# Moving the local exponentials and one chunk's transposes in a hand-planned attention kernel

## The chip, the cores and the metric

The kernel runs on one core of one Trainium2 chip. The time is device microseconds of one execution. Before the change three runs gave 905.56, 906.0 and 906.24 us, median 906.0. The profiled execution took 906.4 us, of which 904.6 us are the span from its first to its last instruction.

## The reference

Two attentions over the same x (2048 positions, width 448, 16 heads of 28) are mixed by a gate per position:

```
q, k, v = x @ A_wqkv                      # A: local and dilated
logits  = q[s] . k[s - 2*w], w = 0..7     # 8 keys per position, masked where s - 2*w < 0
a = (softmax(logits * scale) . v[s - 2*w]) @ A_wo
q, k, v = x @ B_wqkv                      # B: full attention
b = (softmax(q @ k.T * scale) @ v) @ B_wo
out = g * a + (1 - g) * b,   g = sigmoid(sum(x * gate_w))
```

## The kernel before

All is float32, with products split into high and low parts. First come the projections (to about 254 us). Then follow 256 **steps**. The full attention B is cut into 16 units (4 groups of 4 heads by 4 blocks of 512 queries), numbered u = 0 to 15, and each unit into 16 steps kt, one for each block of 128 keys; step st = 16u + kt. In every step TensorE makes the scores of four heads (line 1041), ScalarE turns them into exponentials in two instructions of 128x1024 (line 1044), and TensorE multiplies the exponentials of the step before with V into the bank `av` (line 995). Beside it TensorE makes, up to step 234, three tiles of scores for units to come (line 144), of which VectorE takes the maxima (lines 148 and 174); the maxima go through ScalarE (lines 179, 180), GpSimd (line 181), a VectorE transpose (line 186) and SyncE to DRAM, and serve as the offsets of the later exponentials. The first exponential of a step is taken here as the step's start: step 0 starts at 254.29 us, step 80 at 435.60, step 96 at 471.78.

A unit's output is finished in the steps behind it, at fixed places (`hooks`, filled by `at`): with f = 16(u+1), ScalarE copies `av` to `osb` ahead of the scores of step f+1 (position "pre", line 854), SyncE stores and reloads the row sums, VectorE takes the reciprocal at f+6 (line 867), GpSimd scales it (line 868), SyncE stores it and, at the end of step f+8, loads it back spread over the partitions as `rbc` (line 877); GpSimd multiplies `osb` by `rbc` at the end of step f+12 (`fin_on`, line 906), ScalarE rounds that at "pre" of step f+18 in most units (`fin_hi`, line 910), GpSimd takes the rest (`fin_lo`, line 914), and SyncE stores both at f+22. All DMAs of these steps are issued on SyncE's queue, in program order.

The local attention A runs in the same steps, mostly on GpSimd and VectorE, in 8 **chunks** c = 0 to 7 of two heads (the seventh chunk is c = 6). Its pieces are: loads of q, k and v on SyncE ("ld"); eight products of q with shifted k on GpSimd (`a_score`, item "s", c, w; line 616, for odd w with a folding addition, line 621), each summed by VectorE in 2 or 4 reduces (`a_reduce`, item "r", line 626); a softmax in nine items "m", c, 0 to 8 (`a_softmax`), of which number 4 is the exponential on ScalarE (line 642); eight products with v and seven additions on GpSimd (`a_av`, item "a", c, w, part; lines 665 and 670), of which ("a", c, 7, 1) is the last sum of the chunk; four VectorE transposes (`a_turn`, item "t", line 674); and four pairs of stores on SyncE (`a_store`, "st", line 680).

These pieces are placed by a planner that runs when the program is written out (`issue`). Each engine has a list sorted by a due place. In each step `issue` goes through an engine's list and takes the first item whose needs were issued at least `lag` steps earlier; for GpSimd and VectorE it adds the item's written cost to the engine's backlog `late` and stops when the backlog would pass a limit (4.2 us for GpSimd, 0.7 us for VectorE). At the end of a step the backlog falls by 2.25 us, and VectorE's rises by what the maxima cost. So a placed item changes the room for the items after it, and every later placement can move. Each engine then runs its instructions strictly in the order in which they were written out: in a step first SyncE's items, then GpSimd's, then the scores, VectorE's hooks and items, ScalarE's items, the product with V, and the hooks at "end".

When all items are placed, the output projection's weights are split and the last steps (from 235) take the output products of both attentions.

Of the kernel before, what the change touches and what calls it, by code (L numbers as in the profile page):

```python
# [17 lines left out]
W, DIL = 8, 2  # L18
# [7 lines left out]
def gated_mix_kernel(ctx: ExitStack, tc: tile.TileContext, xT, xn, gw, wA, wB, woAB, out):  # L26
# [179 lines left out]
    with tc.tile_pool(name="xp", bufs=1) as xp, tc.tile_pool(name="wp", bufs=2) as wp:  # L206
# [203 lines left out]
        r, t = xst[:, 0, 0:3, :], xst[:, 0, 3, :]  # L410
# [40 lines left out]
        for n, t in enumerate(tiles):  # L451
# [4 lines left out]
            for w in splits:  # L456
                i, k = (n - splits[w][0]) * splits[w][1], splits[w][1]
# [36 lines left out]
            if parts and parts[0][0] <= n:  # L494
                _, u, t = parts.pop(0)
# [23 lines left out]
    hooks = {}  # L519
# [4 lines left out]
    def run(pos, st):  # L524
        for f in hooks.pop((st, pos), ()):
            f()
# [69 lines left out]
    for nme in ("k", "v"):  # L596
        for i in range(2):
            t = a1.tile([128, HALO + NJ, 56], F32, name=f"{nme}t{i}")
# [3 lines left out]
    def a_load(c, nme):  # L602
        if nme == "q":
            qt[c] = a2.tile([128, NJ, 56], F32, name="qt")
            nc.sync.dma_start(qt[c], a_own[0][c])
        else:
            t = kvt[nme, c % 2]
            i = 1 if nme == "k" else 2
            nc.sync.dma_start(t[:, 0:HALO, :], a_prev[i][c, :, NJ - HALO:NJ, :])
            nc.sync.dma_start(t[:, HALO:, :], a_own[i][c])  # L610

    def a_score(c, w):
        if w == 0:
            Lt[c] = a2.tile([128, W, NJ, 2], F32, name="L", bufs=3)
        p = a3.tile([128, NJ, 56], F32, tag="prod", name="prod")
        nc.gpsimd.tensor_tensor(out=p, in0=qt[c], in1=kvt["k", c % 2][:, HALO - DIL * w:HALO - DIL * w + NJ, :],  # L616
                                op=ALU.mult)
        prods[c, w] = p.rearrange("p j (h d) -> p (j h) d", d=DH)
        if NR[c, w] == 2:
            lo, hi = prods[c, w][:, :, 0:DH // 2], prods[c, w][:, :, DH // 2:]  # L620
            nc.gpsimd.tensor_tensor(out=lo, in0=lo, in1=hi, op=ALU.add)  # L621
            prods[c, w] = lo

    def a_reduce(c, w, i, n):
        r = slice(2 * NJ // n * i, 2 * NJ // n * (i + 1))
        nc.vector.tensor_reduce(Lt[c][:, w].rearrange("p j h -> p (j h)")[:, r], prods[c, w][:, r], axis=X, op=ALU.add)
# [45 lines left out]
    def a_turn(c, i):  # L672
        r = slice(4 * i, 4 * i + 4)
        nc.vector.transpose(oatT[:, r].rearrange("p j h e -> p (j h e)"),
                            oats[c % 2][:, r].rearrange("p j h e -> p (j h e)"))

    def a_store(c, a):
        for h in range(2):
            f = 56 * c + DH * h
            nc.sync.dma_start(oa_scr[f:f + DH].rearrange("f (j p) -> f j p", j=NJ)[:, :, 32 * a:32 * a + 32],  # L680
                              oatT[32 * a:32 * a + DH, :, h, :])
# [6 lines left out]
    def item(eng, key, name, cost, needs, f):  # L688
        lists[eng].append((key, name, cost, needs, f))
# [6 lines left out]
    for c in range(8):  # L696
        c0 = CH * c
        for nme in "qkv":
            item("sp", c0 if nme != "v" else c0 + 18, ("ld", nme, c), 0,
                 [(("s", c - 2, 7), 3)] if nme != "v" else [(("a", c - 2, 7, 1), 3)],  # L700
                 lambda c=c, nme=nme: a_load(c, nme))
        for w, o in enumerate((0, 2, 5, 8, 11, 14, 17, 20)):
            back = (c, w - 4) if w > 3 else (c - 1, w + 4)
            item("pool", c0 + o, ("s", c, w), 2.15 + 0.98 * (NR[c, w] == 2),
                 [(("ld", "k", c), 4), (("ld", "q", c), 4), (("a", c - 3, 7, 0), 0), (("s", c, w - 1), 0)]
                 + ([(last(*back), 0)] if back in NR else []), lambda c=c, w=w: a_score(c, w))
            for i in range(NR[c, w]):
                item("dve", c0 + o + 2 + 0.1 * i, ("r", c, w, i), 0.32,
                     [(("s", c, w), 3), (("r", c, w, i - 1) if i else last(c, w - 1) if w else ("r",), 0)],
                     lambda c=c, w=w, i=i: a_reduce(c, w, i, NR[c, w]))  # L710
        for i, (eng, o, cost, lag) in enumerate((("pool", 22, 0.69, 2), ("dve", 23, 0.35, 3), ("dve", 23.5, 0.35, 0),
                                                 ("pool", 25, 0.69, 1), ("act", 26, 0.3, 3), ("dve", 27, 0.35, 1),
                                                 ("dve", 27.5, 0.35, 0), ("dve", 27.8, 0.36, 0),
                                                 ("pool", 28, 1.14, 1))):
            item(eng, c0 + o, ("m", c, i), cost, [(last(c, 7) if i == 0 else ("m", c, i - 1), lag)],
                 lambda c=c, i=i: a_softmax(c, i))
        n = 0
        for w in range(W):
            for part in ((0,) if w == 0 else (0, 1)):
                item("pool", c0 + 30 + 1.4 * n, ("a", c, w, part), 1.72 if part == 0 else 2.08,  # L720
                     [(("m", c, 8), 0), (("ld", "v", c), 4), (("t", c - 2, 3), 0),
                      (("a", c, w - 1, 1 if w > 1 else 0) if part == 0 else ("a", c, w, 0), 0)],
                     lambda c=c, w=w, part=part: a_av(c, w, part))
                n += 1
        for i in range(4):
            item("dve", c0 + 53 + 0.1 * i, ("t", c, i), 0.43 if c < 7 else 0.35, [(("a", c, W - 1, 1), 1), (("t", c, i - 1), 0)],
                 lambda c=c, i=i: a_turn(c, i))
            item("sp", c0 + 59 + i, ("st", c, i), 0, [(("t", c, 3), 1), (("st", c, i - 1), c < 7)],
                 lambda c=c, i=i: a_store(c, i))
# [5 lines left out]
    def issue(eng, st, limit):  # L735
        q = lists[eng]
        i = 0
        while i < min(len(q), LOOK):
            key, name, cost, needs, f = q[i]
            if any(d in names and issued.get(d, 10 ** 6) + lag > st for d, lag in needs):  # L740
                i += 1
                continue
            if eng in late:
                if late[eng] + cost > limit:
                    return
                late[eng] += cost
            f()
            issued[name] = st
            q.pop(i)
            i = 0  # L750
# [327 lines left out]
    for u in range(NU):  # L1078
        g, b = divmod(u, NB)
        for kt in range(NJ):  # L1080
            st = NJ * u + kt
            if kt == (8 if u < 12 else 12) and u + 1 < NU:
                load_q(u + 1)
            run("pre", st)
            issue("sp", st, 0)
            if st >= A_START:
                issue("pool", st, 4.2)
            if not adone and not lists["pool"]:
                a_done(st)
            if len(adone) == 1 and not any(lists.values()):  # L1090
                a_stored(st)
            cur = {}
            left = s1e - s1c[0]
            for a in scores(u, kt, cur):
                if a == 2:
                    run("mid", st)
            run("dve", st)
            if u and kt == 6:
                late["dve"] += 0.25
            if finished:  # L1100
                v = finished.pop(0)
                t = max_parts(v)
                late["dve"] += 0.3
                late["pool"] += 0.18
                turned = {}
                lag = 2 if v < NU - 1 else 1
                at("dve", st + lag, lambda t=t, w=turned: w.update(r=max_turn(t.bitcast(F32))))
                at("end", st + lag, lambda v=v, w=turned: max_store(v, w["r"]))
            issue("dve", st, DLIM)
            issue("act", st, 0)  # L1110
            run("act", st)
            if prev is not None:
                do_av(prev)
            else:
                for _ in range(2):
                    nc.tensor.matmul(av, KH[0][:, 0:128], KH[0][:, 0:512], start=True, stop=True, skip_group_check=True)
            prev = (kt, cur, g)
            if OPS and st >= OPS[0]:
                op_some(st, (92 * (st - OPS[0] + 1) + 20) // 21 - (92 * (st - OPS[0]) + 20) // 21)
            run("end", st)  # L1120
            step = 2.25 if left else 2.1
            late["dve"] = max(0.0, late["dve"] + 0.58 * min(3, left) - step)
            late["pool"] = max(0.0, late["pool"] - step)
            if st == OP0 + 31:
                op_load_b(2, 3)
            if not OPS and s1c[0] == s1e:
                s1_close()
                OPS.append(st + 1)
# [55 lines left out]
```

## Time and profile before

| | |
|---|---|
| median of 3 runs | 906.0 us |
| profiled execution | 906.4 us |
| its span | 904.6 us |
| TensorE matmul busy | 897.4 us (99%) |
| TensorE weight loads busy | 534.2 us (59%) |
| VectorE busy | 735.3 us (81%) |
| ScalarE busy | 646.1 us (71%) |
| GpSimd busy | 633.7 us (70%) |
| DMA, mean over the span | 115 GB/s |

An engine's busy time says how much of the span it has an instruction in flight. Matmuls are pipelined and their ends are modelled, so 99% for TensorE does not mean that it is at its peak: where another engine holds it up, that shows as a longer step. The length of a step is therefore read from the starts of the exponentials in the timeline of ScalarE.

### The profile page before, as it was taken

The page shows a single profiled execution, that of the slowest core. Times are in us where ns is not written, and L with a number is a line of the kernel's source. Part 1 is how long each engine was busy: PE and PEld are TensorE (multiplying, and loading weights), DVE is VectorE, ACT ScalarE, POOL GpSimd, SP SyncE. Part 2 cuts the span into 40 slices and gives each one's busy share as a digit, 9 for nine tenths or more (in the row PEclk, how much of TensorE's full clock was granted, in tenths as well). Part 3 has the DMA queues.
Part 4 walks back from the last instruction along what each step waited for, and adds up shares of the span by engine and source line. Part 5 has one row for each costly group of instructions (what it writes and reads, how often), then busy time and mean ns, then how long its engine had stood idle before and what let it go on. Part 6 is the DMA issues. An engine that isn't in the chain of part 4 may idle for free.

```text
span 904.6 us, 20583 instructions
## 1 busy us (share of the span) xinstructions
PE 897.4 (99%) x8334; PEld 534.2 (59%) x8334; DVE 735.3 (81%) x989; ACT 646.1 (71%) x775; POOL 633.7 (70%) x502
## 2 busy tenths in 40 slices
PE   9999999999999999999999999999999999999998
PEld 6899999999944444444444444444444444466667
DVE  6488999999989999999999999999999888610012
ACT  6456434443378898898989889888889898855550
POOL 2489847464479799998989999899999389500100
PEclk9999999999999999999999999999999999999999
DMA  9887403554362341245144421523122413455333
GB/s 269 289 264 194 142 12 84 145 133 121 96 245 65 98 119 54 81 108 130 27 120 122 113 89 42 141 66 79 48 82 55 134 26 103 126 155 146 91 95 102
DMA packets 113838, 104.29 MB, mean 115 GB/s; under 512 B 74628, under 2 KB 82180, under 8 KB 112960
## 3 DMA queue, kind: packets, MB, share of 16 engines
q1 hardware_dynamic: 113600, 102.72, 40.2%
q8 instruction: 65, 1.06, 0.5%
q10 hardware_dynamic: 144, 0.26, 0.1%
q14 instruction: 29, 0.24, 0.1%
HBM read 61.99 MB, written 40.48 MB: 113 GB/s over the span
## 4 chain that ended last, share of the span: by engine, by line
PE 92%; POOL 4%; ACT 1%; DVE 1%; DMA 0%; issue 0%; SPq 0%; ACTq 0%; DVEq 0%; POOLq 0%
PE T L1041 28%; PE av L995 26%; PE r L298 15%; PE T L838 8%; PE r L293 8%; PE r L144 5%; PE T L144 4%; POOL oat L670 1%; POOL prod L665 1%; ACT P L1044 1%; DMA raw<-in_wB 0%; POOL prod L616 0%; DVE MX L148 0%; SPq L220 0%; POOL prod L621 0%
## 5 line engine op out<-in xcount | busy, mean ns | idle before, releaser
L1044 ACT ACTIVATE P<-T 128x1024 f32<-128x1024 f32 x512 | 497.2, 1025 | 92.2 <-PE T L1041 91.0
L148 DVE TENSOR_REDUCE MX<-T 128x1 f32<-128x512 f32 x470 | 440.1, 952 | 22.4 <-PE T L144 10.3
L995 PE MATMUL av<-P,V 128*32 128x512 f32 x2048 | 272.7, 605 | 0.4 <-ACT osb L854 0.3
L1041 PEld LDWEIGHTS T<-QH,KH 30*128 30x128 f32 x1024 | 90.6, 181 | 221.4 <-ACT P L1044 196.9
L144 PE MATMUL T<-KH,QP 28*128 28x512 f32 x704 | 219.4, 454 | 0.3 <-DVE MX L162 0.3
L162 DVE TENSOR_REDUCE MX<-r 128x2 f32<-128x1024 f32 x160 | 192.6, 1220 | 24.7 <-PE r L144 23.1
L1041 PE MATMUL T<-QH,KH 30*128 30x512 f32 x1024 | 210.9, 489 | 1.0 <-DVE MX L148 0.8
L1041 PE MATMUL T<-QH,KL 28*128 28x512 f32 x1024 | 185.8, 397 | 0.0
L1041 PE MATMUL T<-QL,KH 28*128 28x512 f32 x1024 | 182.9, 392 | 0.0
L616 POOL TENSOR_TENSOR prod<-qt,kt 128x896 f32<-128x896 f32 x64 | 135.5, 2120 | 0.2
L362 ACT ACTIVATE raw<-r 128x896 f32<-128x896 f32 (+1 forms) x64 | 58.9, 920 | 97.9 <-PE r L298 96.6
L670 POOL TENSOR_TENSOR oat<-oat,prod 128x896 f32<-128x896 f32 x56 | 118.2, 2110 | 2.7
L144 PEld LDWEIGHTS T<-KH,QP 28*128 28x128 f32 x704 | 86.0, 181 | 27.6 <-ACT P L1044 20.9
L363 POOL TENSOR_TENSOR ast<-raw 128x448 f32<-128x448 f32 x48 | 55.4, 1154 | 58.2 <-ACT raw L362 45.8
L665 POOL TENSOR_TENSOR prod<-vt,L 128x896 f32<-128x896 f32 x56 | 95.5, 1705 | 0.6
L1041 PEld LDWEIGHTS T<-QL,KH 28*128 28x128 f32 x1024 | 93.2, 184 | 0.0
L1041 PEld LDWEIGHTS T<-QH,KL 28*128 28x128 f32 x1024 | 91.7, 183 | 1.0
L144 PE MATMUL r<-KH,QP 64*128 64x512 f32 x320 | 86.7, 390 | 0.0
L995 PEld LDWEIGHTS av<-P,V 128*32 128x32 f32 x2048 | 40.3, 108 | 78.1 <-issue 73.1
L298 PE MATMUL r<-wh,xh 64*128 64x448 f32 (+1 forms) x512 | 85.4, 362 | 0.0
L298 PE MATMUL r<-wh,xl 64*128 64x448 f32 (+1 forms) x384 | 70.0, 363 | 0.0
L298 PE MATMUL r<-wl,xh 64*128 64x448 f32 (+1 forms) x448 | 66.1, 367 | 0.0
(120 smaller groups left out, 1038.1 us busy)
## 6 DMA issues: line engine op xcount, KB each, us to landing
a_scr<-ast SPq DMA_DIRECT2D x24, 448.0 KB
qk_hi<-qkh SPq DMA_DIRECT2D x24, 256.0 KB
qk_lo<-qkh SPq DMA_DIRECT2D x24, 256.0 KB
rbc<-rs SPq DMA_DIRECT2D x60, 64.0 KB
QP<-qk_hi SPq DMA_DIRECT2D x64, 56.0 KB
KL<-qk_lo SPq DMA_DIRECT2D x16, 224.0 KB
QH<-qk_hi SPq DMA_DIRECT2D x64, 56.0 KB
QL<-qk_lo SPq DMA_DIRECT2D x64, 56.0 KB
```

The costliest lines, as they stand in the source:

```text
L144: nc.tensor.matmul(bank, qhis[u][h % 2][r, 128 * qs:128 * qs + 128], KH[u // NB % 3][r, 512 * kc:512 * kc + 512], start=True, stop=True)
L148: r = nc.vector.tensor_reduce(MX[:, n % NMX:n % NMX + k], bank, axis=X, op=ALU.max)
L162: nc.vector.tensor_reduce(m, PM[k], axis=X, op=ALU.max)
L293: nc.tensor.matmul(bank, ws[c][rows, k, t[4]:t[4] + 128], x, start=first, stop=last)
L298: nc.tensor.matmul(bank[:, 0:cols], x, ws[c][rows, k, 0:cols], start=first, stop=last)
L616: nc.gpsimd.tensor_tensor(out=p, in0=qt[c], in1=kvt["k", c % 2][:, HALO - DIL * w:HALO - DIL * w + NJ, :], op=ALU.mult)
L665: nc.gpsimd.tensor_tensor(out=dst, in0=kvt["v", c % 2][:, HALO - DIL * w:HALO - DIL * w + NJ, :].rearrange("p j (h d) -> p j h d", d=DH), ...
L670: nc.gpsimd.tensor_tensor(out=oat[c], in0=oat[c], in1=oat[c, w], op=ALU.add)
L838: writes(bank, nc.tensor.matmul(bank[:, :D], src, wo[c][:, k, :], start=(first and k == ks[0] and i == 0), stop=(last and k == ks[-1] and ...
L995: nc.tensor.matmul(av[32 * h:32 * h + 32, :], V[:, kt, 4 * g + h, :], tiles_[h], start=(kt == 0), stop=(kt == NJ - 1), skip_group_check=True)
L1041: nc.tensor.matmul(bank[a], (KH[g % 3], KH[g % 3], KL[g % 2])[t][r, ks], (qh, ql, qh)[t][r, :], start=(t == 0), stop=(t == 2))
L1044: e = nc.scalar.activation(p, RP[0] if a == "2" else mine, AF.Exp, scale=SCALE).ins
```

## The change

Two places change. ScalarE's only items (the eight local exponentials) are not placed in a step whose next step has a hook at "pre" left; such hooks are the copies of a unit's output (`fin_copy`, at f+1) and their rounding (`fin_hi`). And the transposes of chunk 6 may be placed two steps behind the step of the chunk's last sum, where one step was enough; for the other chunks it stays one.

```
-            item("dve", c0 + 53 + 0.1 * i, ("t", c, i), 0.43 if c < 7 else 0.35, [(("a", c, W - 1, 1), 1), (("t", c, i - 1), 0)],
+            item("dve", c0 + 53 + 0.1 * i, ("t", c, i), 0.43 if c < 7 else 0.35, [(("a", c, W - 1, 1), 2 if c == 6 else 1), (("t", c, i - 1), 0)],
...
             issue("dve", st, DLIM)
-            issue("act", st, 0)
+            if (st + 1, "pre") not in hooks:
+                issue("act", st, 0)
             run("act", st)
```

## Rows read from the trace of the kernel before

**Rows 1.** Chain that ended last: shares of the span by engine.

```profile
PE 92%; POOL 4%; ACT 1%; DVE 1%; DMA 0%; issue 0%; SPq 0%; ACTq 0%; DVEq 0%; POOLq 0%
```

**Rows 2.** Waits, 255 to 770 us: engine and line, releaser: us, times, longest.

```profile
PEld T L1041 <- ACT P L1044: 190.2, 227, 1.1
...
DVE nms L186 <- POOL nmt L181: 1.2, 2, 0.9
DVE oatT L674 <- POOL oat L670: 0.9, 1, 0.9
```

**Rows 3.** Timeline of ScalarE, steps 80 to 83: start, duration, instruction, idle before.

```profile
435.60 1.94 ACT L1044 ACTIVATE P<-T 128x1024 f32<-128x1024 f32 x2 [0.38 <-PE T L1041]
...
437.90 1.97 ACT L1044 ACTIVATE P<-T 128x1024 f32<-128x1024 f32 x2
...
442.36 1.94 ACT L1044 ACTIVATE P<-T 128x1024 f32<-128x1024 f32 x2 [0.15 <-PE T L1041]
```

**Rows 4.** Timeline of ScalarE, steps 48 and 49.

```profile
362.96 1.94 ACT L1044 ACTIVATE P<-T 128x1024 f32<-128x1024 f32 x2 [0.18 <-PE T L1041]
364.78 0.42 ACT L642 ACTIVATE L<-L 128x256 f32<-128x256 f32 x1
365.09 0.60 ACT L854 ACTIVATE osb<-av 128x512 f32<-128x512 f32 x1
365.57 1.95 ACT L1044 ACTIVATE P<-T 128x1024 f32<-128x1024 f32 x2
```

**Rows 5.** Timeline of ScalarE, starts of steps 128, 129, 206 and 207.

```profile
544.05 1.94 ACT L1044 ACTIVATE P<-T 128x1024 f32<-128x1024 f32 x2 [0.17 <-PE T L1041]
...
546.66 1.95 ACT L1044 ACTIVATE P<-T 128x1024 f32<-128x1024 f32 x2
...
721.63 1.94 ACT L1044 ACTIVATE P<-T 128x1024 f32<-128x1024 f32 x2 [0.33 <-PE T L1041]
...
724.28 1.94 ACT L1044 ACTIVATE P<-T 128x1024 f32<-128x1024 f32 x2
```

**Rows 6.** Timelines of GpSimd and VectorE at chunk 6's last sum and first transpose.

```profile
703.18 2.12 POOL L670 TENSOR_TENSOR oat<-oat,prod 128x896 f32<-128x896 f32 x1
...
705.34 0.45 DVE L674 STREAM_TRANSPOSE oatT<-oat 128x256 f32<-128x256 f32 x1 [0.95 <-POOL oat L670]
```

**Rows 7.** Timelines of VectorE in step 172 and of ScalarE, starts of steps 173 and 176.

```profile
645.57 0.21 DVE L186 STREAM_TRANSPOSE nms<-nmt 128x32 f32<-128x32 f32 x1 [0.36 <-POOL nmt L181]
...
645.88 1.94 ACT L1044 ACTIVATE P<-T 128x1024 f32<-128x1024 f32 x2 [0.18 <-PE T L1041]
...
653.08 1.94 ACT L1044 ACTIVATE P<-T 128x1024 f32<-128x1024 f32 x2 [0.40 <-PE T L1041]
```

**Rows 8.** Timelines of VectorE in steps 83 and 84, and of SyncE's DMA issues behind them.

```profile
443.94 0.43 DVE L674 STREAM_TRANSPOSE oatT<-oat 128x256 f32<-128x256 f32 x1
...
446.10 0.67 DVE L626 TENSOR_REDUCE L<-prod 128x8 f32<-128x224 f32 x2
...
444.40 3.41 SPq L680 DMA_DIRECT2D oa_scr<-oatT  x4
...
466.58 1.83 SPq L877 DMA_DIRECT2D rbc<-rs  x4
```

**Rows 9.** Timeline of GpSimd, steps 92 to 95.

```profile
464.69 2.11 POOL L616 TENSOR_TENSOR prod<-qt,kt 128x896 f32<-128x896 f32 x1
466.89 1.02 POOL L621 TENSOR_TENSOR prod<-prod 128x448 f32<-128x448 f32 x1
470.12 1.28 POOL L906 TENSOR_TENSOR on<-osb,rbc 128x512 f32<-128x512 f32 x1 [2.21 <-DMA rbc<-rs]
```

**Rows 10.** Timeline of VectorE, the local reduce of step 96.

```profile
473.28 0.38 DVE L626 TENSOR_REDUCE L<-prod 128x16 f32<-128x224 f32 x1
```

**Rows 11.** Timelines of GpSimd and VectorE, step 177.

```profile
655.70 2.12 POOL L670 TENSOR_TENSOR oat<-oat,prod 128x896 f32<-128x896 f32 x1
...
656.75 0.67 DVE L626 TENSOR_REDUCE L<-prod 128x8 f32<-128x224 f32 x2
```

## The prediction

> **What bounds the kernel now.** Read first the chain that ended last: 92% of it is TensorE and 4% GpSimd, while ScalarE and VectorE have 1% each [rows 1]. So time is lost or won only where a step becomes longer or shorter. Then the waits: TensorE's weight loads wait for the exponential of the step before in 227 places, 190.2 us in all [rows 2]. That is the ordinary rhythm of a step and the change doesn't touch it; two small entries, VectorE waiting for GpSimd in a transpose of line 674 (0.9 us) and of line 186 (1.2 us in two places), are the ones to follow [rows 2]. Last, the timeline of ScalarE, from which the length of each step comes. Steps 80, 81 and 82, with a copy and a rounding among them, last 442.36 - 435.60 = 6.76 us together, the first 2.30 [rows 3]. Against that pattern I found five places in steps 4 to 234 that are longer by 0.3 us or more.
>
> - Step 48: 365.57 - 362.96 = 2.61 us. The local exponential of chunk 1 (0.42) and the copy of a unit's output (0.60) stand one behind the other before the next exponential [rows 4]. Excess over 2.30: 0.31.
> - Step 128: the same pair, 546.66 - 544.05 = 2.61, excess 0.31; step 206: the exponential of chunk 7 ahead of a rounding, 724.28 - 721.63 = 2.65, excess 0.35 [rows 5].
> - Steps 198 and 199: chunk 6's first transpose starts at 705.34, as soon as GpSimd's sum has ended (703.18 + 2.12); VectorE had been idle for 0.95 [rows 6]. VectorE is nearly full there, so I take the whole 0.95 as length of a step.
> - Steps 173 to 175: 653.08 - 645.88 = 7.20 against 6.76, excess 0.44, behind a transpose of line 186 that waited for a late GpSimd [rows 7].
>
> **The change part by part.** The guard bars ScalarE's items from step f of every unit (the step ahead of its copy) and, for units 0 to 10, from f+17 (ahead of its rounding; the later units have theirs nearer). Three of the eight local exponentials stand there now (steps 48, 128, 206). I worked the planner's rules through with its written costs, once as they are (the placements agree with the timeline) and once with the two lines changed. Chunk 1's exponential goes from 48 to 50, since 49 is barred by the rounding at 50. This is the only one that the guard moves directly. But the rest of that chunk's softmax and its GpSimd work follow two steps later, GpSimd's list fills its room with other items, and nearly all placements from step 49 on change: the exponentials of chunks 2 to 7 go from 76, 101, 128, 152, 179, 206 to 77, 102, 127, 155, 180, 205. No operation is added or removed; engines' work is the same.
>
> What goes: all eight exponentials stand in allowed steps, so 0.31 + 0.31 + 0.35 go; chunk 6's last sum is placed at 199 instead of 197 and its first transpose at 202 instead of 198, three steps behind, so 0.95 goes; the transpose of line 186 in step 172 depends on how late GpSimd is, and by the new order GpSimd has less in front of it, so I count 0.44 as gone (kept, the sum is 0.44 higher). Gain 2.36 us. An exponential in an allowed step costs nothing as long as ScalarE has its usual idle time of 0.38 or 0.15 in a step to swallow 0.42 of work [rows 3]; without that cover it would be those 0.3 again.
>
> What comes, first place, **step 96**. Chunk 1's transposes move from steps 80 to 83 to 81 to 84, and with them the stores that wait for the last one. SyncE's queue is in order, and behind the first store it now issues DMAs without a gap: 444.40 to 466.58 = 22.18 us for 35 issues, up to the first `rbc` of unit 4, which ends at 466.58 + 1.83 = 468.41 [rows 8]. In front of that `rbc` stand the same 35 issues after the change. The stretch starts with the end of the last transpose: now 443.94 + 0.43 = 444.37; then at VectorE's local place of step 84, 446.10 less the 0.31 saved in step 48, so 445.79 + 0.43 = 446.22, which is 1.85 later [rows 8]. GpSimd's product with `rbc` already waits 2.21 for it, until 470.12, 1.71 after the last issue [rows 9]. It would start at 471.97.
>
> [...]
>
> A wait of GpSimd costs nothing unless someone waits for GpSimd. Now nobody does: product 1 of chunk 4 (2.11 + 1.02 with its folding, 3.22 from 464.69 to 467.91) stands in front of that `rbc` product [rows 9], placed at step 92. With the change it is placed at 93, and so behind it. It would end at 471.97 + 1.23 + 3.22 = 476.42, where 1.23 is what the `rbc` product takes until its follower starts. VectorE's reduces of it are placed three steps later, at 96, as second local item of that step. The first local item of step 96 starts at 473.28 and lasts 0.38 [rows 10]; less 0.31, the second's turn comes at about 473.3. So VectorE stands for 476.42 - 473.3 = 3.1 us, and behind the waiting reduce in its queue are the maxima of step 97, for which TensorE's banks wait. Bounds: if the queue absorbs the shift and `rbc` lands at 470.12 as now, 1.3; if GpSimd isn't held at all, 0; if the queue loses another 1.9 in the same way, 5.0. I take 3.1, because the stretch of issues has no gap that could absorb anything. A reduce in step 99 that is due three steps behind its product takes up to 0.4 more of the same lateness; I take 0.2.
>
> Second place, **step 177**. Chunk 5's last sum stays at step 176, but its first transpose comes from 184 to 177, one step behind, and the longer lag is given to chunk 6 alone. In the trace this very sum, placed in this very step, ends at 655.70 + 2.12 = 657.82, and VectorE's local items of step 177 begin at 656.75 [rows 11]. The transpose would stand for 1.07. Bounds: 0 (GpSimd on time), 2.0 (as late again as it is now). I take 1.07, from the same sum's row.
>
> At the end, chunk 7's last sum is placed at 220 instead of 221 and all stores at 224 instead of 225. The output products start with step 235 in both, so I count nothing (bounds: 0.3 either way, the excess that a collision costs).
>
> Sum: 3.1 + 0.2 + 1.07 - 2.36 = 2.0 us longer. The profiled execution, 906.4 with its span of 904.6, becomes 908.4; the median of the runs stands 0.4 lower, so 906.0 + 2.0 = 908.0.
>
> **The rivals.**
>
> 1. **The stalls go and none comes.** SyncE's stretch behind the stores runs without its slow issues, `rbc` of unit 4 lands before about 468.9 (that is where 3.1 becomes 0), and GpSimd reaches chunk 5's last sum early. For it: GpSimd's lateness changes with every placement, and 22.18 us for 35 issues is 0.63 each, with slow ones among them. Against it: the same stores and loads stand in the same order. Then 906.0 - 2.36 + 0 to 0.5: 903.9. It decides for faster as soon as the two new stalls together stay under 2.36.
> 2. **Half.** `rbc` lands where it does now (1.3 in step 96), 1.07 in step 177: 906.0 + 1.3 + 0.2 + 1.07 - 2.36 = 906.2. For it: a queue that is behind may catch up in its later loads. Against it: no gap to catch up in.
> 3. **The collisions weren't the exponentials' doing**, so that the 0.97 of steps 48, 128 and 206 stays, or GpSimd's greater lateness keeps the 0.44 too: 908.0 + 0.97 + 0.44 = 909.4; with 5.0 in step 96 it is 910 to 911. Against it: the three steps are the only ones with such a pair, and step 80 with a copy alone isn't longer.
>
> **How the numbers follow.** Forecast 0.49, rival 1 0.20, rival 2 0.20, rival 3 0.11. The forecast's own range is 907.0 to 909.3. What a measurement can tell from no change is 0.2%, 1.8 us, so the bounds are 904.2 and 907.8. Faster: rival 1, nearly whole, 0.19. Slower: rival 3 and most of the forecast, 0.49. Within: rival 2 and the forecast's lower end, 0.32. The range reaches from rival 1's time to the near part of rival 3: 903.9 to 909.8.
>
> **What would show it.** Right: steps 48, 128 and 206 at 2.3 us; no wait of line 674 at chunk 6; a wait of VectorE's reduce (line 626) for GpSimd's folding near 473 us with a step of 5 us near 474; GpSimd waiting for `rbc` some 7 us just ahead of it; a transpose of chunk 5 near 657 us that waits about 1 us. Wrong: `rbc` of unit 4 landing by 469 us, no wait of line 626 at all, or the gain of 0.3 us missing in the three steps.

## The result

The changed kernel took 909.64 us (median of 22 runs, 906.32 to 911.88) against 905.68 (22 runs, 905.18 to 907.03): ratio 1.004, 95% interval 1.0032 to 1.0047, so slower by more than 0.2%. The forecast was 908.0, with a range of 903.9 to 909.8. The profiled run is the fastest of the 22, so its page looks much like that of before: matmul busy 99% as it was, the chain with 86% TensorE and 6% GpSimd in place of 92% and 4% [rows 1].

```profile
span 904.2 us, 20585 instructions
PE 896.7 (99%) x8334; PEld 531.9 (59%) x8334; DVE 735.6 (81%) x989; ACT 645.8 (71%) x775; POOL 633.5 (70%) x502
PE 86%; POOL 6%; DMA 2%; SPq 2%; issue 2%; ACT 1%; DVE 1%; POOLq 0%; DVEq 0%; ACTq 0%
```

ScalarE's timeline of that run gives the lengths of the steps:

```profile
363.02 1.94 ACT L1044 ACTIVATE P<-T 128x1024 f32<-128x1024 f32 x2 [0.17 <-PE T L1041]
365.34 1.95 ACT L1044 ACTIVATE P<-T 128x1024 f32<-128x1024 f32 x2
...
473.62 1.95 ACT L1044 ACTIVATE P<-T 128x1024 f32<-128x1024 f32 x2
...
476.72 1.95 ACT L1044 ACTIVATE P<-T 128x1024 f32<-128x1024 f32 x2 [0.64 <-PE T L1041]
...
646.36 1.94 ACT L1044 ACTIVATE P<-T 128x1024 f32<-128x1024 f32 x2 [0.40 <-PE T L1041]
...
653.07 1.94 ACT L1044 ACTIVATE P<-T 128x1024 f32<-128x1024 f32 x2 [0.27 <-PE T L1041]
...
704.98 1.94 ACT L1044 ACTIVATE P<-T 128x1024 f32<-128x1024 f32 x2 [0.31 <-PE T L1041]
707.26 1.94 ACT L1044 ACTIVATE P<-T 128x1024 f32<-128x1024 f32 x2 [0.34 <-PE T L1041]
...
720.75 1.94 ACT L1044 ACTIVATE P<-T 128x1024 f32<-128x1024 f32 x2
...
723.09 4.02 ACT L1044 ACTIVATE P<-T 128x1024 f32<-128x1024 f32 x4
...
756.69 1.94 ACT L1044 ACTIVATE P<-T 128x1024 f32<-128x1024 f32 x2 [0.34 <-PE T L1041]
759.47 0.63 ACT L910 ACTIVATE onhi<-on 128x512 fp32r<-128x512 f32 x1 [0.83 <-POOL on L906]
760.01 4.00 ACT L1044 ACTIVATE P<-T 128x1024 f32<-128x1024 f32 x4
```

Step 199 of the kernel before, for comparison:

```profile
704.91 1.94 ACT L1044 ACTIVATE P<-T 128x1024 f32<-128x1024 f32 x2 [0.23 <-PE T L1041]
708.10 1.94 ACT L1044 ACTIVATE P<-T 128x1024 f32<-128x1024 f32 x2 [1.25 <-PE T L1041]
```

The collisions are gone: step 48 lasts 2.32 us and step 206 2.34, against 2.61 and 2.65 [rows 4, 5]; steps 173 to 175 last 6.71 against 7.20 [rows 7], and step 199 lasts 2.28 against 3.19. Two steps are new among the long ones: the one from 473.62 (step 97; 3.10) and the one from 756.69 (step 222; 3.32).

The next three views are of the same run: SyncE's stretch of issues from the first store to the first `rbc` of unit 4, then GpSimd, then VectorE.

```profile
446.26 1.75 SPq L680 DMA_DIRECT2D oa_scr<-oatT  x2
...
451.74 1.81 SPq L101 DMA_DIRECT2D on_hi<-onhi  x4
...
461.21 1.67 SPq L101 DMA_DIRECT2D QL<-qk_lo  x4
...
465.87 1.95 SPq L877 DMA_DIRECT2D rbc<-rs  x4
```

```profile
469.50 1.28 POOL L906 TENSOR_TENSOR on<-osb,rbc 128x512 f32<-128x512 f32 x1 [5.11 <-DMA rbc<-rs]
470.74 2.11 POOL L616 TENSOR_TENSOR prod<-qt,kt 128x896 f32<-128x896 f32 x1
...
754.37 2.11 POOL L670 TENSOR_TENSOR oat<-oat,prod 128x896 f32<-128x896 f32 x1
756.42 0.56 POOL L772 CAST wo<-rawt 128x448 fp32r<-128x448 f32 x1
...
758.16 1.28 POOL L906 TENSOR_TENSOR on<-osb,rbc 128x512 f32<-128x512 f32 x1
```

```profile
473.99 0.39 DVE L626 TENSOR_REDUCE L<-prod 128x16 f32<-128x224 f32 x1 [0.75 <-POOL prod L621]
...
656.86 0.44 DVE L674 STREAM_TRANSPOSE oatT<-oat 128x256 f32<-128x256 f32 x1
...
713.25 0.44 DVE L674 STREAM_TRANSPOSE oatT<-oat 128x256 f32<-128x256 f32 x1
...
756.51 0.77 DVE L674 STREAM_TRANSPOSE oatT<-oat 128x256 f32<-128x256 f32 x2 [0.61 <-POOL oat L670]
```

The stretch begins at 446.26, 1.86 later than before [rows 8], product 1 of chunk 4 stands behind the `rbc` product, and VectorE's reduce waits for its folding, here only 0.75. Neither chunk 5's first transpose (656.86) nor chunk 6's (713.25, against the 0.95 of [rows 6]) waits.

A profile at 906.3 doesn't explain a median of 909.6. The mean granted clock, which is listed for each run, separates them: 6 of the 22 runs have 0.999 or 1.000 and a median of 906.90; 16 have 0.995 to 0.998 and a median of 910.33. Of the 29 runs of before beside the first experiments none is under 0.999. The experiments ask what makes the wait, what makes the clock fall, and what takes back the gain in the runs in which the clock stays up.

### The profile page after: what moved, and what is told of

Read it like the earlier page. It is cut to its first block, busy times and chain, and to the rows that moved or that the text cites. A ratio compares the mean times of both kernels' runs of the same rounds, so it can differ in the third digit from the quotient of the medians.

```text
span 904.2 us, 20585 instructions
## 1 busy us (share of the span) xinstructions
PE 896.7 (99%) x8334; PEld 531.9 (59%) x8334; DVE 735.6 (81%) x989; ACT 645.8 (71%) x775; POOL 633.5 (70%) x502
## 4 chain that ended last, share of the span: by engine, by line
PE 86%; POOL 6%; DMA 2%; SPq 2%; issue 2%; ACT 1%; DVE 1%; POOLq 0%; DVEq 0%; ACTq 0%
PE T L1041 25%; PE av L995 23%; PE r L298 15%; PE T L838 8%; PE r L293 8%; PE r L144 5%; PE T L144 3%; POOL oat L670 2%; POOL prod L665 2%; SPq L101 1%; DMA rbc<-rs 1%; DMA V<-in_xT 1%; DMA kt<-a_scr 1%; POOL prod L616 0%; ACT P L1044 0%
```

## The experiments

Each was compared with runs of the kernel before on the same chip (medians 905.65 to 905.80). "Low-clock" means runs with a mean granted clock of 0.998 or less.

**Each half alone.** `guard_only` takes the transposes' lag back; `turn_only` takes the guard out.

```
-  (("a", c, W - 1, 1), 2 if c == 6 else 1)
+  (("a", c, W - 1, 1), 1)                                # guard_only
...
-            if (st + 1, "pre") not in hooks:
-                issue("act", st, 0)
+            issue("act", st, 0)                          # turn_only
```

> The guard alone, chunk 6's transposes one step behind its last sum. By the planner's rules all placements are those of the changed kernel but four transposes and their stores (first transpose at step 200, one behind the sum at 199). Theory (the guard reorders GpSimd in steps 92 and 93, and the wait of step 96 is the loss): as slow as the changed kernel, 909.6, plus 0 to 1.0 for a transpose that waits again in step 200, so 909.6 to 910.6. Rival (the loss comes with the seventh chunk's later turn): near or below 906.

> The second line alone: chunk 6's transposes at least two steps behind its last sum, exponentials as before. Placements up to step 198 are those of before, so steps 48, 128 and the 2.21 us wait of GpSimd for rbc near 470 us stay and no reduce waits in step 96. Theory: the 0.95 of step 199 goes, a wait near step 222 may come (chunk 7's last sum one step earlier, its transposes one step behind it, up to 1.0): 904.9 to 906.0, with a narrow spread like before. Rival (the turn is the loss): 908 or more.

`guard_only`: 910.72 (6 runs, 5 low-clock), ratio 1.0048 (1.0034 to 1.0062). In its profile the reduce waits 2.42 and steps 97 and 98 last 4.99 and 3.59. Chunk 6's first transpose doesn't wait, at 711.86:

```profile
475.76 0.39 DVE L626 TENSOR_REDUCE L<-prod 128x16 f32<-128x224 f32 x1 [2.42 <-POOL prod L621]
...
711.86 0.43 DVE L674 STREAM_TRANSPOSE oatT<-oat 128x256 f32<-128x256 f32 x1
```

So the whole loss is the guard's, and beside it the longer lag has nothing left to remove. `turn_only`: 906.07 (11 runs, none low-clock), ratio 1.0003 (0.9994 to 1.0011). Its steps 48 and 128 keep their 2.61, step 199 loses its excess, and step 222 is 3.31 us long, which takes the gain back. Step 206 loses its excess here too (2.35): the lag alone moves chunk 7's exponential from step 206 to 205, so that collision doesn't need the guard.

**Is the order on GpSimd the cause?** `swap` is the changed kernel with unit 4's `rbc` product behind product 1 of chunk 4; `early` issues unit 4's `rbc` loads a step earlier; `flip_before` puts into the kernel before nothing but the changed order of the two products.

```
+        if u == 4:                                                # swap
+            at("end", f + l[4], lambda: pool_time(1.24, lambda: None))
+            at("mid", f + l[4] + 1, lambda u=u: fin_on(u, fin["r"]))
...
+        if u == 4:                                                # flip_before
+            at("end", f + l[4], lambda: pool_time(1.24, lambda: None))
+            at("pre", f + l[4], lambda u=u: fin_on(u, fin["r"]))
...
-        at("end", f + l[3], lambda u=u: fin_spread2(u))
+        at("end", f + l[3] - (u == 4), lambda u=u: fin_spread2(u))  # early
```

> The changed kernel with one GpSimd instruction moved: the product of unit 4 with rbc is written out behind product 1 of chunk 4 instead of ahead of it; every other instruction on every engine stands as in the changed kernel. Theory (VectorE waits in step 96 for a product that stands behind a wait for rbc, and the queue's varying time shows there): the wait of line 626 near 473 us is gone, the median falls by 2.5 to 4 to 905.5 to 907, and the runs agree within about 2 us. Rival (the loss is spread over later waits, or sits in chunk 7's transposes near step 222): 908.5 or more, spread as wide as now.

> The changed kernel with rbc of unit 4 issued one step earlier on SyncE's queue, ahead of twelve... of the offsets' store, the next unit's Q loads and one pair of stores; GpSimd's order is that of the changed kernel. Theory (the queue in front of rbc sets the wait): GpSimd waits for rbc 0 to 1 us instead of 5 or more, no reduce waits in step 96, median 905.5 to 907 with a narrow spread, as with the other order. Rival (GpSimd is late for another reason than rbc): 908.5 or more, and the wait of line 626 stays.

> The kernel before with one GpSimd instruction moved: the product of unit 4 with rbc ahead of product 1 of chunk 4 instead of behind it. Theory (the order of these two alone makes the loss): rbc lands at 470.1, product 1 ends at 474.6 and its reduce, due at 471.3 in step 95, waits 3.3 us; with 0.7 to 1.5 for the clock behind it the median is 909 to 911 and the runs spread over several us. Rival (the shift of the stores by one step is needed too, or many small shifts add up): within 1.5 of before, 905.2 to 907.2.

`swap`: 905.64, ratio 1.0 (0.9991 to 1.0009); `early`: 905.46, ratio 0.9997 (0.9989 to 1.0006); 11 runs each, none low-clock. `flip_before`: 908.51, ratio 1.0027 (1.0017 to 1.0037); of 9 runs 4 have 0.999 or more (median 907.14) and 5 are low-clock (908.80). First GpSimd in `swap`, then GpSimd in `early`, then VectorE in `flip_before`:

```profile
466.28 1.02 POOL L621 TENSOR_TENSOR prod<-prod 128x448 f32<-128x448 f32 x1
471.20 1.28 POOL L906 TENSOR_TENSOR on<-osb,rbc 128x512 f32<-128x512 f32 x1 [3.89 <-DMA rbc<-rs]
```

```profile
464.32 1.28 POOL L906 TENSOR_TENSOR on<-osb,rbc 128x512 f32<-128x512 f32 x1
```

```profile
473.07 0.39 DVE L626 TENSOR_REDUCE L<-prod 128x16 f32<-128x224 f32 x1 [1.28 <-POOL prod L621]
```

In `swap` GpSimd still waits 3.89 for a late `rbc`, but nobody waits for GpSimd, and the 4 us are gone. In `early` the same order as in the changed kernel costs nothing, because `rbc` is there. `flip_before` pays most of the loss without the guard, in step 96 (3.61 us in its profile, of a run at 906.98). In that profile step 199 has lost its excess as well (2.29), with neither guard nor lag: chunk 6's last sum ends at 705.13, as it did before at 705.30, but the steps are later by then and the transpose's turn comes only at 705.80. SyncE's stretch in `flip_before` starts at 444.80, 0.40 later than before, as does its step 96 (472.19 against 471.78), so no later within the step. The reduce's wait for a product that stands behind the `rbc` product is the cause, and its size is set by when `rbc` lands.

**Does the same kernel vary?** `after_again` is the changed kernel, unedited, for a profile of another run.

> The changed kernel once more, for a profile of an execution nearer to the median than the first one (906.3). Theory (slow issues on SyncE's queue fall into the stretch ahead of rbc of unit 4 in most executions; each lengthens the wait of step 96, and behind a wait of some 2.4 us the granted clock fell to 0.5 for 3.4 us in the run with the guard alone): a profile of about 909 to 911 has rbc landing at 470.5 us or later, VectorE's wait near 473 us at 1.8 us or more and the clock at 0.5 for some us behind it. Rival (the slow executions lose elsewhere): rbc lands near 469.5 as in the first profile, the wait is 0.8, and longer steps stand in other places.

908.23 (10 runs, 5 low-clock), ratio 1.0032 (1.0019 to 1.0046); the profiled run took 910.5. Its views follow: SyncE, GpSimd, VectorE, ScalarE, and windows of 2 us. A window's columns are its length, the busy time and count of TensorE, weight loads, VectorE, ScalarE and GpSimd, the granted clock as a share of full speed, the DMA share and GB/s.

```profile
446.21 1.74 SPq L680 DMA_DIRECT2D oa_scr<-oatT  x2
...
451.68 2.46 SPq L101 DMA_DIRECT2D on_hi<-onhi  x4
...
461.81 2.94 SPq L101 DMA_DIRECT2D QL<-qk_lo  x4
...
467.74 1.95 SPq L877 DMA_DIRECT2D rbc<-rs  x4
```

```profile
471.38 1.29 POOL L906 TENSOR_TENSOR on<-osb,rbc 128x512 f32<-128x512 f32 x1 [6.98 <-DMA rbc<-rs]
```

```profile
475.88 0.39 DVE L626 TENSOR_REDUCE L<-prod 128x16 f32<-128x224 f32 x1 [2.67 <-POOL prod L621]
```

```profile
473.61 1.96 ACT L1044 ACTIVATE P<-T 128x1024 f32<-128x1024 f32 x2
...
478.90 1.94 ACT L1044 ACTIVATE P<-T 128x1024 f32<-128x1024 f32 x2 [2.83 <-PE T L1041]
483.19 1.94 ACT L1044 ACTIVATE P<-T 128x1024 f32<-128x1024 f32 x2 [2.34 <-PE T L1041]
```

```profile
475.00:477.00 2.00, 0.45 (x5) 0.13 (x5) 1.12 (x3) 1.07 (x2) 2.00 (x2) 0.96 0.18 36
477.00:479.00 2.00, 1.67 (x11) 1.05 (x13) 1.89 (x3) 0.10 (x1) 2.00 (x3) 0.50 0.92 225
479.00:481.00 2.00, 2.00 (x14) 0.20 (x8) 1.67 (x3) 1.84 (x2) 2.00 (x2) 0.50 0.84 188
481.00:483.00 2.00, 2.00 (x19) 1.18 (x15) 0.76 (x2) 0.00 (x0) 2.00 (x2) 0.50 0.14 29
483.00:485.00 2.00, 2.00 (x22) 0.61 (x18) 1.45 (x3) 1.81 (x2) 1.92 (x2) 0.83 0.06 8
```

The stretch begins where it did in the profile at 906.32, but two groups of four issues take 2.46 and 2.94 in place of 1.81 and 1.67. The 35 issues take 467.74 - 446.21 = 21.53 us, in that profile 465.87 - 446.26 = 19.61. The `rbc` product starts 1.88 later, the reduce waits 2.67 instead of 0.75, and step 97 lasts 5.29. Then the granted clock is 0.50 from 477 to past 483, while TensorE is busy again in nearly the whole of each window, with fewer matmuls. Step 98, in which ScalarE waits 2.34 for TensorE and no reduce for GpSimd, lasts 4.29. The two steps cost 5.29 + 4.29 - 2 x 2.30 = 4.98.

The DMA engines are busy in the windows from 477 to 481 (0.92 and 0.84), but in the changed kernel's run at 906.32 a like burst (0.91) passes at full clock:

```profile
479.00:481.00 2.00, 2.00 (x26) 0.75 (x19) 2.00 (x4) 1.92 (x2) 2.00 (x2) 1.00 0.91 197
```

**How long a wait, without `rbc`?** Three kernels are `early` with unneeded products put on GpSimd behind unit 4's `rbc` product, so that the reduce waits for a busy GpSimd at a chosen time: `hold_short` two of 128x896 and one of 128x448, `hold_long` three and one, `hold_longer` four and none.

```
+        if u == 4:
+            at("end", f + l[4], lambda: hold(2, 1))   # hold_long (3, 1), hold_longer (4, 0)
```

> The changed kernel with rbc of unit 4 issued a step earlier, and GpSimd held instead by fixed work behind its product with rbc: two products of 128x896 and one of 128x448 into unused memory (5.5 us), so that VectorE's wait doesn't depend on the queue. Product 1 of chunk 4 ends at about 474.3, the reduce waits about 1.0. Theory: median 906.3 to 907.0 (905.5 plus the wait), clock at full speed, narrow spread. Rival (each us of wait costs more than itself, whatever its length): 907.5 or more.

> The same with three products of 128x896 and one of 128x448 (7.7 us): the reduce waits about 3.2. Theory (a long wait costs itself and a stretch at half clock): the granted clock falls to 0.5 behind the wait, 905.5 + 3.2 + 1.3 = 909.5 to 911, narrow spread. Rival (the half clock in the run with the guard alone was chance): the clock stays at 1.0 and the median is 908.2 to 909.

> The changed kernel with rbc of unit 4 a step earlier and GpSimd held by four products of 128x896 (8.8 us), so that the reduce waits about 2.7 us, as in the profile of the changed kernel at 910.5 us; the wait doesn't come from the queue here. Theory (a wait of this length costs itself and nearly always a stretch at half clock worth 1.3 to 2): all runs between 908.5 and 911, median 909.5 to 910.5, clock at 0.5 for 3.4 us or more behind the wait. Rival (the clock falls for the queue's or the DMAs' doing, not for the wait): the median is 905.5 + 2.7 = 908.2 or less, clock at 1.0.

| | reduce waits (profile) | median us | ratio (95%) | low-clock runs |
|---|---|---|---|---|
| hold_short | none | 905.74 | 1.0001 (0.9992 to 1.0009) | 0 of 11 |
| hold_long | 1.65 | 907.40 | 1.0022 (1.0014 to 1.0031) | 2 of 11 |
| hold_longer | 2.24 | 909.81 | 1.0041 (1.0028 to 1.0053) | 4 of 5 |

The waits came out shorter than planned (1.0, 3.2 and 2.7), since an unneeded product of 128x896 takes 1.74 us (four of them 6.95 in `hold_longer`), where 2.2 was counted. The profiled run of `hold_long` is one of its two low-clock ones, at 909.38; the nine others have a median of 907.25. Windows of it, with the same columns as above:

```profile
479.00:481.00 2.00, 2.00 (x12) 0.51 (x8) 1.29 (x3) 1.19 (x2) 2.00 (x2) 0.50 0.91 201
481.00:483.00 2.00, 2.00 (x23) 0.83 (x16) 1.32 (x2) 0.86 (x1) 2.00 (x2) 0.77 0.38 78
```

Here, where unneeded products and not `rbc` made GpSimd late, a wait of that size cost about its own length (1.65 in the profile; 907.25 against `early`'s 905.46 is 1.79), and the two runs in which the clock fell took 1.78 more (median 909.03). Behind 2.24 it fell in 4 of 5 runs, behind 1.65 in 2 of 11. Why it falls in one run and not in another of the same kernel isn't shown.

**What takes the gain back at step 222?** In the changed kernel all local work ends a step earlier, and the split of the output weights (lines 772 and 773) slips in on GpSimd between chunk 7's last sum and unit 12's `rbc` product, whose rounding ScalarE then waits for. `early_last_two` and `turn_last_two` let chunk 7's transposes too be two steps behind the sum; `early_split_later` is the first of these with the splits one step later.

```
-  (("a", c, W - 1, 1), 2 if c == 6 else 1)
+  (("a", c, W - 1, 1), 2 if c in (6, 7) else 1)   # early_last_two, turn_last_two, early_split_later
...
-            at("act", st + k, lambda k=k: split_wo(k))
+            at("act", st + 1 + k, lambda k=k: split_wo(k))        # early_split_later
```

> The changed kernel with rbc of unit 4 issued a step earlier, and with the longer lag for chunk 7's transposes as well (first of them at step 222 instead of 221, its stores at 225 as in the kernel before). Theory: the wait of line 674 near 756 us (0.6, step 222 at 3.3) goes as well; what the guard was to give is then left over: 905.46 less 0.6 to 1.0 = 904.5 to 904.9, below before beyond the interval. Rival (the step of 3.3 comes from the weights' splits or the rounding in the same step): no gain, 905.3 to 905.6.

> The kernel before with the longer lag for chunks 6 and 7 and no guard: the three collisions in steps 48, 128 and 206 stay, both waits of line 674 go. Theory: 906.07 less 0.6 to 1.0 = 905.1 to 905.5, some 0.6 above the kernel that has the guard, the earlier rbc and both lags. Rival (the exponentials' collisions cost nothing at the end): the same time as that kernel.

> The kernel with the guard, rbc of unit 4 a step earlier and the longer lag for chunks 6 and 7, and now with the splits of the output weights started one step later, so that on GpSimd the product of unit 12 with rbc follows chunk 7's last sum at once, with no split between. Theory (the step of 3.3 at 222 is ScalarE's rounding waiting for that product, 0.82): the product ends 1.7 us earlier, the rounding doesn't wait, step 222 takes 2.3 to 2.4, median 904.5 to 905.0, below before beyond the interval. Rival (something else in that step is next in line, or a later wait takes the gain): 905.3 to 905.8.

`early_last_two`: 905.72, ratio 0.9998 (0.9989 to 1.0007); `turn_last_two`: 906.23, ratio 1.0004 (0.9995 to 1.0013); `early_split_later`: 904.95, ratio 0.999 (0.998 to 0.9999); 11 runs each, none low-clock. ScalarE at step 222 in `early_last_two`, then in `early_split_later`:

```profile
755.90 1.94 ACT L1044 ACTIVATE P<-T 128x1024 f32<-128x1024 f32 x2 [0.34 <-PE T L1041]
758.67 0.63 ACT L910 ACTIVATE onhi<-on 128x512 fp32r<-128x512 f32 x1 [0.82 <-POOL on L906]
759.21 1.92 ACT L1044 ACTIVATE P<-T 128x1024 f32<-128x1024 f32 x2
```

```profile
755.89 1.94 ACT L1044 ACTIVATE P<-T 128x1024 f32<-128x1024 f32 x2 [0.37 <-PE T L1041]
757.71 0.63 ACT L910 ACTIVATE onhi<-on 128x512 fp32r<-128x512 f32 x1
758.24 1.94 ACT L1044 ACTIVATE P<-T 128x1024 f32<-128x1024 f32 x2
```

My first reading of step 222 was the transpose's wait of 0.61. That reading fell: `early_last_two` removes that wait and the step still lasts 3.31. With the split behind the `rbc` product it lasts 2.35, and the median falls by 0.77. `turn_last_two` is 0.51 above `early_last_two`, though not for three collisions, as was expected. Its steps 48 and 128 keep their 2.61, but step 206 lasts 2.35 as in all kernels with the longer lag. The 0.51 is of the size of what steps 48, 128 and 173 to 175 (6.89 against 6.72) lose here. Both kernels missed the gain that was expected of them, since step 222 stayed long in both (3.31 and 3.33).

`early_split_later` is the change with its two new waits taken out. It is 0.1% below the kernel before, and its interval ends just short of 1; that is less than the 0.2% that I count as a difference.

## Why the prediction was right, and where it wasn't

The side, the place and the main mechanism were right. In the sum of 2.0 the size of step 96 was that of one run, the clock's part was missing, and two errors of about 1 us cancelled.

1. **The gains** (counted 2.36). In the fastest run: step 48 0.29, step 206 0.31, steps 173 to 175 0.49, step 199 0.91. Step 128 lost 0.33, and the step ahead of it, where the exponential now stands, took 0.13 of that back. Held in sum, less so in its causes. The 0.95 of chunk 6 went with the guard's new order alone (`guard_only`) as well as with the lag alone (`turn_only`), and so did step 206's excess. Of the 0.49 only some 0.2 is the change's: `turn_only`, `turn_last_two` and `flip_before`, whose local work stands there as it did before, last 6.94, 6.89 and 6.92 in steps 173 to 175, so the 7.20 was partly that one run's.
2. **Step 96** (counted 3.1, and 0.2 behind it). The mechanism held in every link: the stretch 1.86 later (1.85 was worked out), `rbc` at 471.38 in `after_again` (471.97), the folding behind it, the reduce waiting 2.67 (3.1). With the measured starts of the `rbc` product, 469.50 and 471.38, the prediction's own working gives waits of 0.65 and 2.53 (start + 1.23 + 3.22 - 473.3); 0.75 and 2.67 were measured. The size isn't one number: 0.75, 2.42 and 2.67 us in three profiles of this order, by how long two groups of SyncE's issues take. "The stretch of issues has no gap that could absorb anything" held, but its length of 22.18 [rows 8] was that of one run; 19.61, 21.23 and 21.53 were seen since. From the end of the last issue to the product it took 1.68 and 1.69, as the 1.71 of [rows 9]. Counted from that issue's start, 0.42 earlier, it is 2.11 in both.
3. **The clock** (counted nothing). This is the largest miss. The mean clock was low in 16 of 22 runs, the windows of `after_again` show its fall right behind the wait (0.96 from 475 to 477, then 0.50), and step 98 cost 1.99 there. That takes the pair to 4.98. That this is the upper bound of 5.0 is chance: there a longer queue was meant.
4. **Step 177** (counted 1.07). It didn't come. Chunk 5's last sum started at 654.64 instead of 655.70 [rows 11] and had ended, 654.64 + 2.10 = 656.74, before the transpose at 656.86. The step failed where it took the sum's lateness from its row of before though GpSimd's order ahead of it was another; the bound of 0 held.
5. **The end** (counted nothing, bounds 0.3). Step 222 cost 1.02. I had asked when the last pieces end, and not what is released by their end: the weight split, which came in front of unit 12's `rbc` product.

With the measured sizes the low-clock run of `after_again` is 4.98 + 1.02 - 2.2 = 3.8 longer than the profiled run of before, and its span is: 908.4 against 904.6. For the fastest run it is 0.8 + 1.02 - 2.2 = -0.4, and the spans are 904.2 and 904.6. So the steps named here make up the difference between these profiles to within 0.1 us. From the median of before it would be 905.68 + 3.8 = 909.5, where the low-clock runs' median is 910.33. Most of that gap of 0.8 is that the profiled run of before, 906.4, is 0.7 above its median; why it is stays open. The missing 1.07 and the 1.02 that wasn't counted cancelled, which is luck; the clock put the median above the forecast. It is luck, too, that 909.64 lies inside the range: the forecast's own part ended at 909.3, and the rest up to 909.8 was there for rival 3. The second rival's time (906.2) is near that of the fastest runs, but by other terms: there the `rbc` product starts at 469.50, near the 470.12 that it assumed, since the stretch was shorter, and 1.02 in step 222 stands in for the 1.07 of step 177. Rival 3's times (909.4 to 911) are those of the other runs, but not by its cause, since the collisions did go.

## What to carry to other kernels

When a planner moves one small item, follow each place where two engines' queues meet: here a 0.3 us gain moved a product behind one that waits for a late DMA, and the cure was to issue that DMA one step earlier. Price a wait on TensorE's feed with its length and with the clock that may fall behind it (in `hold_long` 1.79 us, and 1.78 more in 2 runs of 11). And when work ends earlier, look at what its end releases.

## What the runs showed of the hardware

Where VectorE's reduce waited 1.65 us (`hold_long`), 2.24 (`hold_longer`), 2.42 (`guard_only`) and 2.67 (`after_again`), windows with a granted clock of 0.50 followed in the profile; behind 0.75 (the changed kernel) and 1.28 us (`flip_before`) it stayed at 1.00. Five of `flip_before`'s nine runs are low-clock, and none of these has a profile. The windows of 2 us show 1.00 and 0.50, with values between (0.56 to 0.96) only in windows next to one at 0.50.

SyncE's issues are not of one length: four loads took 1.67 us in one run and 2.94 in another of the same kernel, with the same issues ahead of them. They and one group of four stores are the slow ones in `guard_only` too (2.69 and 2.40), and were so before (3.10 and 3.03). In the three profiles of the changed order the stretch took 19.61, 21.23 and 21.53 us, and the reduce waited 0.75, 2.42 and 2.67. That this, with the low clock behind the longer waits, is what spreads the changed kernel's 22 runs over 5.6 us is argued from these three, not shown. Why single issues are slow was not tried and stays open.
